# Products of zeros in TensorE's waits ahead of the first FFN group

## The chip, the cores and the metric

The kernel runs on one core of one Trainium2 chip. The metric is the device time of one execution in microseconds (us), as the median of several runs. The core's engines work side by side, each through its own queue in order: TensorE (PE in the profile; its weight loads are PEld), VectorE (DVE), ScalarE (ACT), GpSimd (POOL) and SyncE (SP). They wait for each other by semaphores, and the 16 DMA engines move data between HBM and the on-chip memory. TensorE writes its results to PSUM, which this kernel uses as eight banks of 128 x 512 float32.

TensorE's clock is granted by a throttle. The profile shows it as a share of full speed, 1.00 or 0.50 here.

## What is computed

Sliding-window attention with an ALiBi bias (8 batches, 8 heads, 576 positions, head size 64, window 128), and then a gated FFN over the 4608 resulting tokens:

```python
scores = scale * np.matmul(q, k.transpose(0, 1, 3, 2))
bias = slopes[:, None, None] * (-np.abs(rel).astype(np.float32))[None, :, :]
mask = (rel >= 0) & (rel < window)
scores = np.where(mask, scores + bias[None], -1000000000.0)
attn = np.exp(scores)            # after the row maximum was taken off
attn = attn / (np.sum(attn, axis=-1, keepdims=True) + 1e-09)
x = np.matmul(attn, v)           # then as 4608 tokens x 512
g = x @ w_gate                   # 512 x 1536
gelu = 0.5 * g * (1.0 + erf(g * inv_sqrt2))
out = (gelu * (x @ w_val)) @ w_out   # 1536 x 512
```

Inputs and output are float32 in HBM. The kernel computes in bfloat16 with float32 sums.

## The kernel before

The first FFN group of 512 tokens needs the attention of batch 0, and nothing can be computed before the first rows of q and k have landed. So the kernel has an opening, in which batch 0 goes through its stages with little beside it, and then a long steady part, in which the attention of later batches is spread between the FFN's products. The change touches only the opening. Its building blocks:

```python
def bank():                                   # one PSUM bank, from a pool of 8
    return psum.tile([128, 512], FP32, name="ps")

def transpose_runs(n, what, c, ps):           # q or k of two heads, on TensorE
    ...
            nc.tensor.transpose(out=ps[...], in_=src[...], identity=ident[...])

def scores(b, s, cs, then=None):              # for the head pairs in cs
    pss = []
    for c in cs:
        ps = [bank(), bank()]
        pss.append(ps)
        ...                                   # score(): qT x kT into the two banks
    if then:
        then()                                # more TensorE work, ahead of the exps
    for c, ps in zip(cs, pss):
        P = p_pool[s].tile([128, 2, 512], BF16, name="P")
        for i in (0, 1):
            exp(P[:, i, :], ps[i])            # ScalarE, L170
        mask(P..., emask...)                  # VectorE, L173: times exp(bias) and mask

def sums(b, s):                               # row sums: P x ones on TensorE, L221
    ps = bank()
    ...
    nc.vector.reciprocal(sumrow[b][:, lo:hi], ps[:, 0:hi - lo])         # L230

def spread_pe(b, s):                          # 1/sum to all partitions, L244
    pss = [bank() for _ in range(4)]
    ...                                       # four float32 products with sel
    for c, ps in enumerate(pss):
        copy = nc.scalar.copy if c % 2 == 0 else nc.vector.tensor_copy
        copy(out=recip[b][:, c, lo:hi], in_=ps[:, 0:hi - lo])           # L251

def values(b, s, cs):                         # P x v on TensorE, L262
    ...
    for c, ps in zip(cs, pss):
        nc.vector.tensor_tensor(out=xT[:, c, ...], in0=ps[...],
                                in1=recip[b][:, c, lo:hi], op=ALU.mult) # L268

def gate_val(g, f, lo=0, hi=512):             # gate and value of 128 FFN columns
    pg, pv = bank(), bank()
    ...                                       # 4 + 4 products with xT, L281
    nc.scalar.activation(out=gl, in_=pg, func=AF.Gelu)                  # L285
    nc.vector.tensor_tensor(out=hid[g][:, f, lo:hi], in0=pv, in1=gl, op=ALU.mult)  # L286
```

In `scores`, `s` is the part of the batch: 0 is positions 0 to 319, 1 is 320 to 575. The opening is this (the loads and constants ahead of it are cut down to what bears on the change):

```python
load_runs(0, 0, 4)                            # first rows of q and k, heads 0 to 3
nc.vector.memset(ident, 0.0)
...                                           # further memsets, masks, loads
for h in range(H):                            # emask: eight activations, L346
    nc.scalar.activation(out=emask[:, h, :], in_=tmpl, func=AF.Exp, scale=-slope)

def first(cs):
    for w in (0, 1):                          # q, then k
        for c in cs:
            ps = bank().bitcast(BF16)
            transpose_runs(0, w, c, ps)
            untangle(act if c == 3 else dve, 0, w, c, ps)   # copy to qT or kT, L136

def rest(cs, copy): ...                       # the same for the last 192 positions

first((0, 1))
scores(0, 0, (0, 1), lambda: first((2,)))
first((3,))
scores2(0)                                    # the middle blocks of all head pairs
scores(0, 0, (2, 3), lambda: rest((0, 1), dve))
scores(0, 1, (0, 1), lambda: sums(0, 0))
rest((2, 3), act)
scores(0, 1, (2, 3))
spread_pe(0, 0)
values(0, 0, range(4))
sums(0, 1)
for f in range(2):
    gate_val(0, f, 0, 320)
spread_pe(0, 1)
gate_val(0, 2, 0, 320)
values(0, 1, range(4))
for f in range(3):
    gate_val(0, f, 320, 512)
...
```

After that come the gates f = 3 to 11 of group 0 in full width, and the steady part.

Of the kernel before, what the change touches and what calls it, by code (L numbers as in the profile page):

```python
# [7 lines left out]
FP32 = mybir.dt.float32  # L8
BF16 = mybir.dt.bfloat16
# [17 lines left out]
def kernel(  # L27
# [10 lines left out]
    nc = tc.nc  # L38
# [11 lines left out]
    consts = ctx.enter_context(tc.tile_pool(name="consts", bufs=1))  # L50
# [9 lines left out]
    psum = ctx.enter_context(  # L60
        tc.tile_pool(name="psum", bufs=8, space=bass.MemoryType.PSUM))

    def bank():
        return psum.tile([128, 512], FP32, name="ps")

    wg = consts.tile([128, 4, DFF], BF16, name="wg")
    wv = consts.tile([128, 4, DFF], BF16, name="wv")
# [27 lines left out]
    def runs(t, n):  # L95
        first, parts, r = RUNS[n]
        lo = 1536 * n
        return t.rearrange("p j x -> p (j x)")[0:parts, lo:lo + 512 * r].rearrange(
            "p (h x) -> p h x", h=H)

    def load_runs(n, h0, h1):
        first, parts, r = RUNS[n]
        for t, src in ((qs[0], q), (ks[0], k)):
            nc.gpsimd.dma_start(  # L104
                out=runs(t, n)[:, h0:h1, :],
                in_=src[0][h0:h1, first:first + parts * r, :].rearrange(
                    "h (p r) d -> p h (r d)", r=r))
# [14 lines left out]
    def transpose_runs(n, what, c, ps):  # L122

        first, parts, r = RUNS[n]
        src = runs((qs, ks)[what][0], n)
        for x in range(r):
            for i in (0, 1):
                nc.tensor.transpose(
                    out=ps[64 * i:64 * i + 64, parts * x:parts * x + parts],
                    in_=src[:, 2 * c + i, 64 * x:64 * x + 64],  # L130
                    identity=ident[0:parts, 0:parts])

    def untangle(copy, n, what, c, ps):
        first, parts, r = RUNS[n]
        dst = by_pair((qT, kT)[what][0])[:, c, 64 + first:64 + first + parts * r]
        copy(out=dst.rearrange("p (x r) -> p x r", r=r),  # L136
             in_=ps[:, 0:parts * r].rearrange("p (r x) -> p x r", r=r))

    def transpose(b, what, c, copy):
        ps = bank().bitcast(BF16)  # L140
        for j in range(5):
            nc.tensor.transpose(  # L142
                out=ps[:, 128 * j:128 * j + 128],
                in_=(qs, ks)[what][b][:, j, 128 * c:128 * c + 128], identity=ident)
        copy(out=(qT, kT)[what][b][:, :, c, :],
             in_=ps[:, 0:640].rearrange("p (j t) -> p j t", t=128))
# [15 lines left out]
    def score(b, c, i, j, qj, n, ps, col):  # L162
        nc.tensor.matmul(  # L163
            out=ps[:, col:col + 128 * n].rearrange("p (n t) -> p n t", n=n),
            lhsT=blocks(kT, b, i, c, j, 1).rearrange("p n t -> p (n t)"),
            rhs=blocks(qT, b, i, c, qj, n),
            start=True, stop=True)

    def exp(dst, src):
        nc.scalar.activation(out=dst, in_=src, func=AF.Exp, scale=0.125)  # L170

    def mask(dst, m):
        nc.vector.tensor_tensor(out=dst, in0=dst, in1=m, op=ALU.mult)  # L173

    def scores2(b):

        P = p2_pool.tile([128, 4, 2, 128], BF16, name="P2")
        probs2[b] = P
        ps = [bank(), bank()]
        for c in range(4):  # L180
            for i in (0, 1):
                score(b, c, i, 2, 2, 1, ps[i], 128 * c)
        for i in (0, 1):
            exp(P[:, :, i, :], ps[i].rearrange("p (c n) -> p c n", c=4))
        mask(P.rearrange("p c i n -> p (c i) n"), emask[:, :, 0:128])

    def scores(b, s, cs, then=None):
# [6 lines that stand above are left out]
            for j, qj, n, col in (((0, 0, 2, 0), (1, 1, 2, 256)),  # L194
                                  ((4, 4, 1, 0), (2, 3, 1, 128), (3, 3, 2, 256)))[s]:
                for i in (0, 1):
                    score(b, c, i, j, qj, n, ps[i], col)
        if then:
            then()
        for c, ps in zip(cs, pss):  # L200
            P = p_pool[s].tile([128, 2, 512], BF16, name="P")
            probs[b, s, c] = P
            for i in (0, 1):
                exp(P[:, i, :], ps[i])
            mask(P.rearrange("p i (n x) -> p i n x", n=2),
                 emask[:, 2 * c:2 * c + 2, :].unsqueeze(2).to_broadcast((128, 2, 2, 256)))

    def prob(b, s, c, i, j, n):
        if (s, j) == (0, 2):
            return probs2[b][:, c, i, 0:n]  # L210
        return probs[b, s, c][:, i, PCOL[s][j]:PCOL[s][j] + n]
# [3 lines left out]
    def sums(b, s):  # L215

        ps = bank()
        for j, a, e in PIECES[s]:
            for i in (0, 1):
                for c in range(4):  # L220
                    nc.tensor.matmul(  # L221
                        out=ps[32 * c:32 * c + 32, a:e],
                        lhsT=ones[:, min(j, 1), i, :], rhs=prob(b, s, c, i, j, e - a),
                        start=(i == 0 and j == 2 * s), stop=(i == 1 and j == 2 * s + 2),
                        skip_group_check=True)
        if s == 0:
            sumrow[b] = r_pool.tile([128, S], FP32, name="r")
            recip[b] = r_pool.tile([128, 4, S], FP32, name="rb")
        lo, hi = PART[s]
        nc.vector.reciprocal(sumrow[b][:, lo:hi], ps[:, 0:hi - lo])  # L230
# [9 lines left out]
    def spread_pe(b, s):  # L240
        lo, hi = PART[s]
        pss = [bank() for _ in range(4)]
        for c, ps in enumerate(pss):
            nc.tensor.matmul(  # L244
                out=ps[:, 0:hi - lo],
                lhsT=sel[32 * c:32 * c + 32, :, :].rearrange("p i m -> p (i m)"),
                rhs=sumrow[b][32 * c:32 * c + 32, lo:hi], start=True, stop=True,
                tile_position=(32 * c, 0))
# [4 lines that stand above are left out]
    def values(b, s, cs):  # L253
        lo, hi = PART[s]
# [4 lines that stand above are left out]
            for j, a, e in PIECES[s]:  # L259
                for i in (0, 1):  # L260
                    h = 2 * c + i
                    nc.tensor.matmul(  # L262
                        out=ps[64 * i:64 * i + 64, a:e],
                        lhsT=vb[b % 2][:, j, 64 * h:64 * h + 64],
                        rhs=prob(b, s, c, i, j, e - a),
                        start=(j == 2 * s), stop=(j == 2 * s + 2), skip_group_check=True)
        for c, ps in zip(cs, pss):
            nc.vector.tensor_tensor(  # L268
                out=xT[:, c, b * S + lo:b * S + hi], in0=ps[:, 0:hi - lo],
                in1=recip[b][:, c, lo:hi], op=ALU.mult)  # L270
# [34 lines left out]


    load_runs(0, 0, 4)
    nc.vector.memset(ident, 0.0)
    for t in (qT[0], kT[0]):
        nc.vector.memset(by_pair(t)[:, :, 0:64], 0.0)  # L310
# [2 lines left out]
        out=ident, in_=ident, compare_op=ALU.not_equal, fill=1.0,  # L313
# [5 lines left out]
    for half, base, step, chan in ((0, 0, 1, -1), (1, -1, -1, 1)):  # L319
        t = tmpl[:, 128 * half:128 * half + 128]  # L320
        nc.gpsimd.affine_select(
            out=t, in_=t, compare_op=ALU.is_ge, fill=1e9,
            base=base, pattern=[[step, 128]], channel_multiplier=chan)
    load_runs(1, 0, 8)
    for c in range(4):
        nc.gpsimd.affine_select(
            out=sel, in_=sel, compare_op=ALU.not_equal, fill=1.0,
# [22 lines left out]
    act, dve = nc.scalar.copy, nc.vector.tensor_copy  # L350
    def first(cs):
        for w in (0, 1):
            for c in cs:
                ps = bank().bitcast(BF16)
                transpose_runs(0, w, c, ps)
                untangle(act if c == 3 else dve, 0, w, c, ps)

    def rest(cs, copy):
        for c in cs:
            for w in (0, 1):  # L360
                ps = bank().bitcast(BF16)
                transpose_runs(1, w, c, ps)
                untangle(copy, 1, w, c, ps)

    first((0, 1))
    scores(0, 0, (0, 1), lambda: first((2,)))
    first((3,))
    scores2(0)
    scores(0, 0, (2, 3), lambda: rest((0, 1), dve))
    scores(0, 1, (0, 1), lambda: sums(0, 0))  # L370
    rest((2, 3), act)
    scores(0, 1, (2, 3))
    spread_pe(0, 0)
    values(0, 0, range(4))
    sums(0, 1)
# [7 lines left out]
    for n in range(2):  # L383
        nc.gpsimd.dma_start(
            out=wo[:, 6 * n:6 * n + 6, :],
# [93 lines left out]
```

The softmax here doesn't subtract the row's maximum and nothing guards it: scores larger than these inputs give would overflow.

## Time and profile before

| | |
|---|---|
| median of 3 runs | 367.69 us (367.64 to 367.73) |
| span of the profiled execution | 365.5 us |
| granted TensorE clock, mean of the span | 0.985 |
| first product on TensorE | 5.05 us after the span's start |
| first gate products | 23.33 us |

The span runs from the first to the last instruction of the profiled execution. A page of the profile gives the busy time of each engine, and then the same in 40 slices (9.1 us each here), where a digit is the busy share in tenths and PEclk is the granted clock in tenths. A chain of waits follows the work that ended last back to what released each step. Other views list one engine's instructions in order of time, the busy time in chosen stretches, and groups of equal instructions with their mean duration. A busy TensorE isn't TensorE at its peak: products are pipelined, and at half the clock the same work is busy for longer.

### The profile page before, as it was taken

How to read it: one execution, taken by the hardware profiler on the slowest of the kernel's cores; microseconds unless marked ns; L12 is line 12 of the kernel's file. 1: busy time of each engine (PE TensorE's matmuls, PEld its weight loads, DVE VectorE, ACT ScalarE, POOL GpSimd, SP SyncE). 2: the span in 40 equal slices, each digit the busy share in tenths (PEclk: the TensorE clock that was granted, in tenths of full speed). 3: DMA queues.
4: the chain of work that ended last, by engine and by line, in shares of the span. 5: the costliest groups of instructions: out<-in, count | busy, mean ns of one | idle time of the engine just before them, and what ended most of it. 6: DMA issues, size and time to landing. Idle time of an engine off the chain costs nothing.

```text
span 365.5 us, 6601 instructions
## 1 busy us (share of the span) xinstructions
PE 347.8 (95%) x2614; PEld 171.3 (47%) x2656; DVE 188.6 (52%) x306; ACT 187.3 (51%) x339; POOL 107.9 (30%) x140
## 2 busy tenths in 40 slices
PE   3799999999999999999999999999999999999995
PEld 2455545444454445444445444444444444444442
DVE  4794448543695469475547454655564404302320
ACT  5863487434966376943783368436842223323321
POOL 8945859913519202900850040000000000000000
PEclk9779999999999999999999999999999999999999
DMA  9999999999969994999991992094205020011002
GB/s 103 136 199 178 177 163 184 174 153 200 162 116 121 136 92 81 143 103 217 127 196 50 228 97 89 33 221 53 87 32 131 0 109 7 0 60 58 0 29 88
DMA packets 151168, 41.41 MB, mean 113 GB/s; under 512 B 138816, under 2 KB 144448, under 8 KB 151136
## 3 DMA queue, kind: packets, MB, share of 16 engines
q0 software_dynamic: 112608, 18.88, 67.8%
q1 hardware_dynamic: 38528, 22.10, 27.2%
q8 instruction: 21, 0.34, 0.4%
q14 instruction: 11, 0.09, 0.1%
HBM read 42.47 MB, written 9.51 MB: 142 GB/s over the span
## 4 chain that ended last, share of the span: by engine, by line
PE 86%; ACT 5%; DVE 3%; DMA 3%; issue 1%; POOL 1%; POOLq 0%; SPq 0%; ACTq 0%; DVEq 0%
PE ps L281 50%; PE ps L297 23%; PE ps L262 4%; ACT P L170 4%; PE ps L163 4%; DMA qT<-qs 3%; PE ps L221 2%; PE ps L244 2%; DVE r L230 1%; DVE P L173 1%; DVE xT L268 1%; ACT emask L346 1%; PE ps L142 1%; POOL ks L104 0%; ACT L170 0%
## 5 line engine op out<-in xcount | busy, mean ns | idle before, releaser
L286 DVE TENSOR_TENSOR hT<-ps,gelu 128x512 bf16<-128x512 f32 (+2 forms) x111 | 74.3, 674 | 121.9 <-PE ps L281 109.3
L285 ACT ACTIVATE gelu<-ps 128x512 bf16<-128x512 f32 (+2 forms) x111 | 64.9, 585 | 119.6 <-PE ps L281 117.2
L281 PE MATMUL ps<-xT,wg 128*128 128x512 bf16 (+2 forms) x430 | 110.6, 374 | 0.8
L281 PE MATMUL ps<-xT,wv 128*128 128x512 bf16 (+2 forms) x435 | 110.4, 373 | 0.6
L297 PE MATMUL ps<-wo,hT 128*128 128x512 bf16 x413 | 97.2, 380 | 1.5 <-issue 0.6
L170 ACT ACTIVATE P<-ps 128x512 bf16<-128x512 f32 x144 | 74.4, 632 | 7.1 <-PE ps L163 7.0
L281 PEld LDWEIGHTS <-wv 128*128 128x128 bf16 x444 | 43.3, 98 | 50.3 <-issue 0.2
L281 PEld LDWEIGHTS <-wg 128*128 128x128 bf16 x444 | 41.9, 98 | 48.9 <-issue 1.1
L173 DVE TENSOR_TENSOR P<-P,emask 128x1024 bf16<-128x1024 bf16 x72 | 48.3, 685 | 31.3 <-ACT P L170 31.0
L297 PEld LDWEIGHTS <-hT 128*128 128x128 bf16 x432 | 39.8, 98 | 49.0 <-issue 4.4
L84 POOL DMA_DIRECT2D vb<-in_v_dram x40 | 33.7, 862 | 75.8 <-PE ps L262 75.0
L302 ACT COPY osb<-ps 128x512 f32<-128x512 f32 x36 | 21.7, 603 | 37.2 <-PE ps L297 32.8
L84 POOL DMA_DIRECT2D qs<-in_q_dram x35 | 29.6, 877 | 24.9 <-DMA qT<-qs 12.9
L230 DVE RECIPROCAL r<-ps 128x320 f32<-128x320 f32 (+1 forms) x16 | 30.7, 1939 | 3.1 <-PE ps L221 3.1
L84 POOL DMA_DIRECT2D ks<-in_k_dram x35 | 29.6, 887 | 6.4 <-DMA qs<-in_q_dram 3.0
L163 PE MATMUL ps<-qT,kT 64*128 64x256 bf16 (+1 forms) x384 | 24.0, 254 | 3.0 <-DVE kT L136 1.3
L268 DVE TENSOR_TENSOR xT<-ps,rb 128x320 bf16<-128x320 f32 (+1 forms) x64 | 24.7, 449 | 0.8 <-DMA rb<-rd 0.8
L163 PEld LDWEIGHTS <-kT 64*128 64x128 bf16 x384 | 13.1, 96 | 16.9 <-issue 11.6
L262 PE MATMUL ps<-P,vb 128*64 128x128 bf16 (+2 forms) x384 | 19.4, 251 | 0.1
L262 PEld LDWEIGHTS <-vb 128*64 128x64 bf16 x384 | 15.4, 113 | 7.3 <-issue 7.2
L221 PE MATMUL ps<-P,ones 128*32 128x128 bf16 (+2 forms) x384 | 11.6, 256 | 1.3 <-DVE P L173 1.3
L221 PEld LDWEIGHTS <-ones 128*32 128x32 bf16 x384 | 8.5, 101 | 5.6 <-issue 4.5
(47 smaller groups left out, 91.3 us busy)
## 6 DMA issues: line engine op xcount, KB each, us to landing
out_dram<-osb SPq DMA_DIRECT2D x36, 256.0 KB, 2.7
rb<-rd SPq DMA_DIRECT2D x8, 576.0 KB, 7.1
vb<-in_v_dram POOLq DMA_DIRECT2D x32, 128.0 KB, 4.7
qs<-in_q_dram POOLq DMA_DIRECT2D x28, 128.0 KB, 6.7
ks<-in_k_dram POOLq DMA_DIRECT2D x28, 128.0 KB, 6.4
wg<-in_moe_w_gate_dram POOLq DMA_DIRECT2D x4, 384.0 KB, 11.0
wv<-in_moe_w_val_dram POOLq DMA_DIRECT2D x4, 384.0 KB, 12.2
wo<-in_moe_w_out_dram POOLq DMA_DIRECT2D x2, 768.0 KB, 10.9
```

The source lines that it names most:

```text
L84: nc.gpsimd.dma_start(out=t[lo:128, j, :].rearrange("p (h d) -> p h d", h=H), in_=src[b][:, 128 * j - 64 + lo:128 * j + 64, :].rearrange(" ...
L163: nc.tensor.matmul(out=ps[:, col:col + 128 * n].rearrange("p (n t) -> p n t", n=n), lhsT=blocks(kT, b, i, c, j, 1).rearrange("p n t -> p ( ...
L170: nc.scalar.activation(out=dst, in_=src, func=AF.Exp, scale=0.125)
L173: nc.vector.tensor_tensor(out=dst, in0=dst, in1=m, op=ALU.mult)
L221: nc.tensor.matmul(out=ps[32 * c:32 * c + 32, a:e], lhsT=ones[:, min(j, 1), i, :], rhs=prob(b, s, c, i, j, e - a), start=(i == 0 and j == ...
L230: nc.vector.reciprocal(sumrow[b][:, lo:hi], ps[:, 0:hi - lo])
L262: nc.tensor.matmul(out=ps[64 * i:64 * i + 64, a:e], lhsT=vb[b % 2][:, j, 64 * h:64 * h + 64], rhs=prob(b, s, c, i, j, e - a), start=(j == ...
L268: nc.vector.tensor_tensor(out=xT[:, c, b * S + lo:b * S + hi], in0=ps[:, 0:hi - lo], in1=recip[b][:, c, lo:hi], op=ALU.mult)
L281: nc.tensor.matmul(out=ps[:, 0:hi - lo], lhsT=w[:, c, 128 * f:128 * (f + 1)], rhs=xT[:, c, t0 + lo:t0 + hi], start=(c == 0), stop=(c == 3))
L285: nc.scalar.activation(out=gl[:, 0:hi - lo], in_=pg[:, 0:hi - lo], func=AF.Gelu)
L286: nc.vector.tensor_tensor(out=hid[g][:, f, lo:hi], in0=pv[:, 0:hi - lo], in1=gl[:, 0:hi - lo], op=ALU.mult)
L297: nc.tensor.matmul(out=po, lhsT=hid[g][:, f, 128 * t:128 * (t + 1)], rhs=wo[:, f, :], start=(f == 0), stop=(f == NF - 1))
```

## The change

A tile of zeros, 128 x 512 in bfloat16, is added, and a helper that issues a given number of products of zeros ahead of the next bank's real work. Each has 128 x 128 zeros as its weights and 512 columns of zeros, and writes to the bank that the real work then overwrites (`start=True`), so the results stay what they were. There are 26 of them: 9 ahead of the first transposes of q, 2 ahead of those of k, 2 ahead of the first scores, 1 ahead of the transposes of the third head pair, 2 ahead of the scores of the last two pairs, 4 ahead of the first scores of part 1, 2 ahead of the sums, 1 ahead of the last scores, and 3 ahead of the first spread. They are meant to fill TensorE's waits ahead of the first FFN group, so that the throttle doesn't halve its clock there. Nothing is taken away.

```diff
+    heat = [0]
+
     def bank():
-        return psum.tile([128, 512], FP32, name="ps")
+        ps = psum.tile([128, 512], FP32, name="ps")
+        for _ in range(heat.pop()):
+            nc.tensor.matmul(out=ps, lhsT=zeros[:, 0:128], rhs=zeros, start=True, stop=True)
+        heat.append(0)
+        return ps
+
+    def keep_busy(n):
+        heat[0] = n
...
     load_runs(0, 0, 4)
+    zeros = consts.tile([128, 512], BF16, name="zeros")
+    nc.vector.memset(zeros, 0.0)
     nc.vector.memset(ident, 0.0)
...
     def first(cs):
         for w in (0, 1):
+            if w and len(cs) == 2:
+                keep_busy(2)
             for c in cs:
...
+    keep_busy(9)
     first((0, 1))
-    scores(0, 0, (0, 1), lambda: first((2,)))
+    keep_busy(2)
+    scores(0, 0, (0, 1), lambda: (keep_busy(1), first((2,))))
     first((3,))
     scores2(0)
+    keep_busy(2)
     scores(0, 0, (2, 3), lambda: rest((0, 1), dve))
-    scores(0, 1, (0, 1), lambda: sums(0, 0))
+    keep_busy(4)
+    scores(0, 1, (0, 1), lambda: (keep_busy(2), sums(0, 0)))
     rest((2, 3), act)
+    keep_busy(1)
     scores(0, 1, (2, 3))
+    keep_busy(3)
     spread_pe(0, 0)
     values(0, 0, range(4))
     sums(0, 1)
```

## The prediction

> **What bounds the kernel now.** I read the page's busy shares first. TensorE is the bound over the whole span.
>
> ```profile
> span 365.5 us, 6601 instructions
> PE 347.8 (95%) x2614; PEld 171.3 (47%) x2656; DVE 188.6 (52%) x306; ACT 187.3 (51%) x339; POOL 107.9 (30%) x140
> PEclk9779999999999999999999999999999999999999
> ```
>
> The clock row has a dent in slices 2 and 3 (9 to 27 us), and this is what the change aims at. An average over a stage says little, so next I read the stretches of this opening. Columns: stretch and length, then busy us with instructions of PE, PEld, DVE, ACT, POOL, then the granted clock.
>
> ```profile
> 10.00:13.40 3.40, 1.85 (x34) 1.16 (x32) 2.17 (x6) 3.08 (x8) 3.40 (x5) 0.99 1.70 118
> 13.40:16.80 3.40, 2.79 (x44) 1.78 (x46) 2.19 (x7) 3.04 (x6) 3.40 (x6) 0.50 1.75 129
> 16.80:20.20 3.40, 2.89 (x34) 1.39 (x30) 3.40 (x4) 3.04 (x8) 2.06 (x3) 0.50 1.24 182
> 20.20:23.60 3.40, 3.40 (x54) 2.49 (x51) 3.40 (x9) 2.05 (x4) 1.58 (x2) 0.50 1.29 197
> 23.60:27.00 3.40, 3.40 (x29) 2.16 (x28) 2.95 (x5) 1.42 (x4) 1.49 (x2) 1.00 1.31 203
> ```
>
> The clock is halved from 13.4 to 23.6 us, 10.2 us in all, and the drop follows a stretch in which TensorE was busy for 1.85 of 3.40 us. Yet ACT was busy for 3.08 and 3.04 us of the stretches around the drop, and DVE for all 6.8 us from 16.8 to 23.6. A halved clock costs time only where TensorE is what the others wait for. So the view that decides is the chain of waits through this opening (start us, length us, what):
>
> ```profile
> 5.77 2.56 ACT emask L346 x8
> 8.33 1.93 ACT P L170 x4
> ...
> 14.20 1.21 DVE P L173 x2
> 15.41 0.04 issue
> 15.46 1.13 PE ps L221 x19
> 16.59 0.02 issue
> 16.61 2.17 DVE r L230
> 18.78 0.14 issue
> 18.91 1.45 PE ps L244 x8
> 20.37 2.06 PE ps L262 x24
> 22.43 0.97 PE ps L221 x19
> 23.40 2.40 PE ps L281 x16
> 25.80 0.64 PE ps L244 x8
> ```
>
> Up to 15.4 us the chain is ScalarE and VectorE. From 15.46 it alternates: row sums on TensorE, a reciprocal on VectorE, then 5 us of TensorE at half clock. A naive reading halves every TensorE piece of that. The timeline of VectorE shows a second chain just beside it, and this is the step on which my number turns:
>
> ```profile
> 18.68 2.43 DVE L173 TENSOR_TENSOR P<-P,emask 128x1024 bf16<-128x1024 bf16 x4
> 21.03 0.88 DVE L251 COPY rb<-ps 128x320 f32<-128x320 f32 x2
> 21.83 1.68 DVE L268 TENSOR_TENSOR xT<-ps,rb 128x320 bf16<-128x320 f32 x4
> ```
>
> The reciprocal, four masks, two copies and four products stand in this order in VectorE's queue and run without a gap from 16.61 to 23.51 us. The first gate products (from 23.33) need all four of these products' results.
>
> [...]
>
> One warning on the clock figure: it reads 1.00 from the start, but the groups of instructions deny that. A score of 256 columns took 404 ns between 5 and 10 us, 269 ns between 10 and 13.3, and 417 ns between 13.7 and 23.3. So TensorE was slow up to about 10 us as well, for which the trace just has no record.
>
> **The change, part by part.** *Added:* 26 products of 512 columns, 9+2+2+1+2+4+2+1+3, and one memset of 128x512 bf16 (the 64x512 bf16 memsets took 0.27 us). Nothing is removed, and no transfer is touched. At full clock the fill costs 26 x 0.216 = 5.6 us of TensorE, at half clock 11.2 us.
>
> *The nine* stand ahead of the first transposes, for which TensorE now waits until 5.05 us on the load of q. The memset can be done near 1.1 us; at half clock nine take 9 x 0.432 = 3.9 us, so they end about when the load lands: cost up to 0.1 us. *The next two* fill the 0.29 us wait on k. [...] ScalarE has the eight emask activations until 8.33 anyway, so a first score by 8.3 costs nothing.
>
> *The next nine* (2+1+2+4) stand where ScalarE and VectorE set the pace: ten activations run from 11.33 to 16.44 without a gap, and the masks end at 15.41. The fill takes 0.2 to 0.9 us at a time, in waits of 0.68, 0.99 and 0.2 us and the slack of a faster clock. I count 0. *Two* ahead of the sums: at full clock the last scores are done by about 14.75, the zeros by 15.2, and the sums wait on the mask at 15.41 either way.
>
> *What the clock gives.* The 21 sums take 1.12 us now; the same 21 at full clock, in a later group, took 0.66. So the reciprocal starts 0.46 us earlier, at 16.15. The next scores wait on ScalarE's copies, whose start moves from 16.92 to about 16.5; *one* zero fits there. The last scores end near 17.7, the *three* zeros take 0.65 and end at 18.35, and the reciprocal ends at 16.15 + 2.17 = 18.32. So spread starts at about 18.45 instead of 18.91 and takes 0.75 (a later group) instead of 1.45. The values and sums shrink by about 1.0 and 0.4 us. TensorE alone would gain 0.46 + 0.70 + 1.03 + 0.42 = 2.6 us, and some more in the first gates.
>
> But VectorE's queue moves by 0.46 us and no more: its products end at 23.51 - 0.46 = 23.05. The first gate's fourth product waits for that, then 0.135 us a product at full clock (320 columns; 4 in 0.54): the three remaining sets of four of f=0 and f=1 run from 23.2 to 24.82. Before, the second spread started at 25.73. VectorE's second reciprocal (1.76 us) now runs from 23.0 to 24.75, so spread starts at about 24.9. Gain: 25.73 - 24.9 = 0.83 us. Behind it everything was already at full clock and TensorE leads: the gain is carried on.
>
> *Is it lost later?* The weights: GpSimd's wait on the landing of the first wv quarter ends at 22.50, and its first use moves from 24.00 to 23.2: 0.7 us left. The k of the next batch: its small packets end near 40.3 us, its transposes start at 41.9: 1.6 us left. wo lands 9.4 and 12.3 us after its issues at 36.7 and 37.6, and the two halves are first used at 50.6 and after 52.9. The transfers behind q's transposes of the third batch land at 84.8 and are used at 90.1. None is eaten up by 0.8 us. So 367.69 - 0.83 + about 0.05 for the nine and the three that end a little late = 366.9.
>
> **Rivals.** *Whole TensorE gain (2.6 us or more, 365.0).* For it: the chain names TensorE for most of 15.5 to 26 us. Against it: VectorE has no gap from 16.61 to 23.51, and its work gets no faster with TensorE's clock. *The fill doesn't hold the clock.* In the stretch from 10.0 to 13.4 the scores and transposes stream about 1.0 us of columns; the two zeros and two of the four add 0.86, making 1.9 of 3.4. The stretch from 16.8 to 20.2 had TensorE busy for 2.89 us and the clock stayed halved, so I can't exclude that 1.9 is too little. Then the four zeros take 1.7 us instead of 0.9 and delay the scores by about 0.9, and the three take 1.3 and push spread from 18.9 to about 20: slower by 1 to 1.5 us, 369. *The start is late.* If the clock comes up only at 8 us, the eleven zeros at half clock delay the first scores beyond 8.33, and ScalarE's unbroken chain moves by 0.3 to 0.5 us: 367.3. *Full clock, but the shift meets a load:* 0.7 us of weights' slack caps it; no change to the point.
>
> **Range and chances.** About 65% for the clock held and VectorE as the limit (366.4 to 367.2), 15% for the late start or a part of the fill on the path (367.2 to 367.9), 17% for a clock that still falls (367.9 to 369), and a few per cent for more than 1.4 us. So 366.9, and 8 in 10 between 366.1 and 368.2. A change of 2% is 7.35 us; the fill at half clock throughout is 11 us but over half of it in waits, and all that the clock could give is half of 10.2 us. Hence 0.01 faster, 0.98 within, 0.01 slower.
>
> **What would show it.** Right: a clock of 1.00 from 13.4 to 23.6; the first reciprocal near 16.1 and its masks, copies and products gapless to about 23.0; spread for the second part near 24.9; the continuous gates from 31.77 starting near 31.0. Wrong: VectorE idle ahead of its products with xT (TensorE still leads, or fill on the path); a clock of 0.50 anywhere after 8 us; the first P activations after 8.4 us; TensorE waiting for wv or for ks that it did not wait for.

## The result

The changed kernel takes 366.86 us (median of 6 runs, 366.56 to 367.72) against 367.72 us for the kernel before beside it (367.64 to 367.99): a ratio of 0.9977, interval 0.9965 to 0.9990. It is faster by about 0.86 us, 0.2%, as the prediction of 366.9 us had it.

The page after:

```profile
span 364.9 us, 6652 instructions
PE 351.6 (96%) x2638; PEld 170.7 (47%) x2682; DVE 189.0 (52%) x307; ACT 187.2 (51%) x339; POOL 108.1 (30%) x140
PEclk9999999999999999999999999999999999999999
```

The dent in the clock row is gone. TensorE is busy for 3.8 us more (351.6 against 347.8), which is not useful work: the fill adds to its busy time, and the real work, at the whole clock, takes less (the first spread 0.82 us instead of 1.45). The same stretches as before, with the same columns (stretch, length, busy PE, PEld, DVE, ACT, POOL, clock):

```profile
13.40:16.80 3.40, 3.33 (x58) 1.62 (x56) 2.65 (x7) 3.40 (x9) 3.40 (x6) 1.00 1.72 124
16.80:20.20 3.40, 3.24 (x45) 1.81 (x47) 3.40 (x5) 3.35 (x10) 2.29 (x4) 1.00 1.28 190
20.20:23.60 3.40, 2.37 (x37) 1.22 (x34) 3.40 (x8) 1.37 (x2) 1.39 (x2) 1.00 1.31 202
```

In the last stretch TensorE, which was busy throughout before, is busy for 2.37 of 3.40 us. It got its work done sooner and waits. What for stands in its timeline (start, length, engine, line, operation; in brackets the idle time before and what ended it):

```profile
18.50 0.82 PE L255 MATMUL ps<-r,sel 32*128 32x320 f32 x8
...
20.36 0.96 PE L232 MATMUL ps<-P,ones 128*32 128x128 bf16 x24
22.02 1.40 PE L292 MATMUL ps<-xT,wg 128*128 128x320 bf16 x4 [0.69 <-DVE xT L279]
...
24.97 0.71 PE L255 MATMUL ps<-r,sel 32*128 32x256 f32 x8
```

The first four gate products waited 0.69 us for xT, and then were drawn out over 1.2 us, since each needs the next product of VectorE. VectorE's queue after:

```profile
16.17 2.16 DVE L241 RECIPROCAL r<-ps 128x320 f32<-128x320 f32 x1 [0.74 <-PE ps L232]
18.25 2.43 DVE L184 TENSOR_TENSOR P<-P,emask 128x1024 bf16<-128x1024 bf16 x4
20.59 0.88 DVE L262 COPY rb<-ps 128x320 f32<-128x320 f32 x2
21.39 1.68 DVE L279 TENSOR_TENSOR xT<-ps,rb 128x320 bf16<-128x320 f32 x4
```

Set against the times of before (16.61, 18.68, 21.03 and 21.83 us), each start is 0.43 or 0.44 us earlier and each length is the same. The whole clock moved the start of this queue, by the shorter sums (all 24 in 0.99 us, where the last 21 alone took 1.12 before), and nothing else in it. The lead at the second spread is 25.73 - 24.97 = 0.76 us. It doesn't all reach the end. The chain of waits further on, after (start, length, what):

```profile
31.02 10.09 PE ps L292 x46
41.11 0.68 PE ps L153 x10
...
42.06 1.46 PE ps L292 x6
```

Before, the same steps were these:

```profile
31.77 10.09 PE ps L281 x46
41.86 0.56 PE ps L142 x10
...
42.69 1.46 PE ps L281 x6
```

The lead is 0.75, 0.75 and then 0.63 us: ten transposes of batch 1's q and k, which took 0.56 us before, take 0.68. From there on the lead stays at 0.62 to 0.63 us to the end of the chain, and the two spans differ by as much (365.5 and 364.9).

### The profile page after: what moved, and what is told of

It is laid out like the page before. It is cut to its first block, busy times and chain, and to the rows that moved or that the text cites. A ratio compares the mean times of both kernels' runs of the same rounds, so it can differ in the third digit from the quotient of the medians.

```text
span 364.9 us, 6652 instructions
## 1 busy us (share of the span) xinstructions
PE 351.6 (96%) x2638; PEld 170.7 (47%) x2682; DVE 189.0 (52%) x307; ACT 187.2 (51%) x339; POOL 108.1 (30%) x140
## 4 chain that ended last, share of the span: by engine, by line
PE 86%; ACT 8%; DVE 2%; issue 1%; POOL 1%; POOLq 0%; ACTq 0%; DVEq 0%
PE ps L292 50%; PE ps L308 23%; ACT P L181 6%; PE ps L273 4%; PE ps L174 4%; PE ps L232 2%; PE ps L255 1%; DVE xT L279 1%; DVE P L184 1%; ACT L181 1%; ACT emask L359 1%; PE ps L153 1%; DVE r L241 0%; POOL ks L115 0%; ACT osb L313 0%
## 5 line engine op out<-in xcount | busy, mean ns | idle before, releaser
L273 PE MATMUL ps<-P,vb 128*64 128x128 bf16 (+2 forms) x384 | 18.4, 243 | 0.1
L232 PE MATMUL ps<-P,ones 128*32 128x128 bf16 (+2 forms) x384 | 10.8, 243 | 1.3 <-DVE P L184 1.1
```

Of the source, the lines that this page charges most:

```text
L232: nc.tensor.matmul(out=ps[32 * c:32 * c + 32, a:e], lhsT=ones[:, min(j, 1), i, :], rhs=prob(b, s, c, i, j, e - a), start=(i == 0 and j == ...
L273: nc.tensor.matmul(out=ps[64 * i:64 * i + 64, a:e], lhsT=vb[b % 2][:, j, 64 * h:64 * h + 64], rhs=prob(b, s, c, i, j, e - a), start=(j == ...
```

## The experiments

The theory: with the clock held, VectorE's queue sets when the first gates come, and a part of what is won is taken back where batch 1's k has not landed yet. The rival: TensorE is the only limit, so that the fill brought all that the clock can give. All ratios are to the kernel before on the same chip, with 95% intervals. The runs are from more than one chip, on which the kernel before took 367.84 us (rows 2 to 5), 367.75 us (the two halves and the last two rows) and 367.59 us (the other three), so medians of different groups can be compared only roughly.

| kernel | median us (range, runs) | ratio |
|---|---|---|
| changed kernel | 366.86 (366.56 to 367.72, 6) | 0.9977 (0.9965 to 0.9990) |
| + late transposes | 366.79 (366.52 to 367.58, 11) | 0.9974 (0.9964 to 0.9983) |
| + VectorE relieved | 366.85 (366.14 to 367.31, 8) | 0.9970 (0.9958 to 0.9981) |
| + both | 365.57 (365.25 to 368.90, 14) | 0.9944 (0.9928 to 0.9959) |
| no fill, both | 367.80 (367.09 to 368.70, 14) | 0.9996 (0.9987 to 1.0005) |
| + late transposes, mask only | 366.39 (366.27 to 366.89, 6) | 0.9959 (0.9943 to 0.9975) |
| + late transposes, copies only | 366.00 (365.77 to 366.51, 5) | 0.9951 (0.9937 to 0.9965) |
| only the early fill | 367.73 (367.01 to 368.09, 13) | 0.9995 (0.9987 to 1.0003) |
| only the late fill | 368.02 (366.55 to 368.68, 14) | 1.0004 (0.9992 to 1.0016) |
| six ahead of the spread | 366.78 (366.56 to 367.49, 8) | 0.9977 (0.9967 to 0.9987) |
| half of the columns | 367.05 (366.54 to 368.17, 22) | 0.9979 (0.9971 to 0.9987) |
| transposes as fill | 367.17 (366.54 to 368.30, 18) | 0.9982 (0.9973 to 0.9991) |

### Late transposes

```diff
-            if g == 0 and f >= 8:
+            for c in {9: (0,), 10: (1, 2), 11: (3,)}.get(f, ()) if g == 0 else ():
                 for w in (0, 1):
-                    transpose(1, w, f - 8, (act, dve)[w])
+                    transpose(1, w, c, (act, dve)[w])
```

> With the fill, and the transposes of batch 1's q and k one gate later (after gates 9, 10, 10 and 11 instead of 8 to 11). If the k load takes back a part of the gain (in the changed kernel TensorE was 0.75 us ahead at 31 us and 0.63 us from 42 us on) and is also what makes its runs scatter by 1.1 us: the 0.75 us stay to the end, about 366.6 us to 366.8, and the runs lie within 0.4 us. Rival, the 0.12 us are something else and the scatter is the clock's: 366.9 and a scatter as before.

366.79 us: too near to the changed kernel to tell 0.12 us by the medians. In the profile the transposes take 0.56 us again. No view of the changed kernel's profile names a wait on a load at these transposes, so that the load of k took back the 0.12 us is inferred here; the next experiment shows the wait itself. The runs scatter by 1.1 us as before, not within 0.4 us: this load is not what makes them scatter.

### VectorE relieved

```diff
-    scores(0, 1, (0, 1), lambda: (keep_busy(2), sums(0, 0)))
+    later = []
+    scores(0, 1, (0, 1), lambda: (keep_busy(2), sums(0, 0, later)), lambda: later[0]())
...
-            copy = nc.scalar.copy if c % 2 == 0 else nc.vector.tensor_copy
+            copy = nc.scalar.copy if c % 2 == 0 or (b, s) == (0, 0) else nc.vector.tensor_copy
```

In the helpers, `sums` puts its reciprocal into `later`, and `scores` calls it after its first mask.

> With the fill, and VectorE relieved by about 1.4 us in the opening: one mask goes ahead of the reciprocal into VectorE's wait, and two copies of the first spread go to ScalarE. If VectorE's queue held back the first gates: their fourth product starts near 21.8 instead of 23.1 us, the value product then waits for the load of wv at 22.0 to 22.5, the second spread comes near 24.2 instead of 24.97, 0.75 us earlier; but then batch 1's k isn't there at 40.5, TensorE waits for it until 41.2, and nearly nothing is left: 366.5 to 366.9 us. Rival, TensorE alone set the end: no change of the second spread, 366.9 us. Second rival, no wait on k: 366.1 us.

366.85 us, no better than the changed kernel, and yet the rival falls by the profile: the second spread starts at 23.95 instead of 24.97, 1.0 us earlier. This is where that went, in the timeline of TensorE:

```profile
23.95 0.71 PE L260 MATMUL ps<-r,sel 32*128 32x256 f32 x8
...
40.20 0.53 PE L153 MATMUL ps<-ident,ks 128*128 128x128 bf16 x3
41.38 0.23 PE L153 MATMUL ps<-ident,ks 128*128 128x128 bf16 x1 [0.66 <-DMA ks<-in_k_dram]
42.22 0.23 PE L153 MATMUL ps<-ident,ks 128*128 128x128 bf16 x1 [0.60 <-DMA ks<-in_k_dram]
```

TensorE came 1.0 us earlier to k's transposes (40.20 instead of 41.23) and waited 1.26 us there. The profiled run, at 367.31 us, is the longest of the eight, and the shortest took 366.14 us, so not every run need lose all of it; the median does. An experiment read by its time alone would have said that VectorE doesn't matter.

### Both

The two edits together, nothing else.

> Both: VectorE relieved, and the transposes one gate later. If VectorE's queue and then the k load are the two limits: about 1.5 us ahead of the kernel before, 366.1 to 366.3 us. If the k load isn't a limit: the same as the relief alone. If VectorE isn't: the same as the late transposes alone, 366.7 us.

365.57 us, better than expected: 0.9944 is 2.1 us of 367.84 (2.3 by the medians). One of the 14 runs took 368.90 us. The mean clock recorded for it is 0.995, the lowest of the 14, so the clock may have fallen in it; no profile of that run is kept. The chain of waits of the profiled run shows VectorE for 1.3 us only:

```profile
20.85 1.28 DVE xT L284 x3
...
22.17 1.93 PE ps L297 x13
24.10 0.64 PE ps L260 x8
...
30.07 10.74 PE ps L297 x49
```

The long run of gates starts at 30.07 us, 0.95 earlier than in the changed kernel, though the first P activation came 0.2 us later in this run; and nothing takes it back. With the late transposes in both, VectorE's relief is worth 366.79 - 365.57 = 1.22 us; without them, nothing that the runs can tell (0.9970 against 0.9977, with intervals that overlap).

### Both, without the fill

> The kernel before, without the fill, with VectorE relieved and the transposes one gate later. If TensorE's half clock and VectorE's queue end within 0.1 to 0.3 us of each other there, relief alone gives little: the clock stays halved from 13.4 to 23.6 us, 367.4 to 367.7 us. Rival, VectorE alone was the limit and the clock hardly matters: 1 us or more is gained without any fill, 366.7 us or less.

367.80 us, a ratio of 0.9996 with 1 inside its interval. The clock in its stretches:

```profile
16.80:20.20 3.40, 2.90 (x45) 1.78 (x37) 3.00 (x3) 2.67 (x9) 2.44 (x4) 0.50 1.27 184
20.20:23.60 3.40, 3.40 (x52) 2.22 (x48) 2.95 (x6) 3.25 (x7) 1.24 (x2) 0.50 1.31 201
```

Now VectorE has gaps (3.00 and 2.95 us busy of 3.40) and TensorE has none at the end. So at half the clock TensorE's own work sets the end once VectorE is relieved, and the two had ended close together before. From the first product of the first sums to the second spread this kernel takes 26.33 - 15.38 = 10.95 us, and the kernel before took 25.73 - 14.80 = 10.93 us: no gain. The clock alone brought 0.9 us, VectorE's relief and the late transposes without it nothing that can be told from 0, and all together 2.1 to 2.3.

### The two halves of the relief

Only the mask ahead of the reciprocal, or only the two copies on ScalarE, each with the fill and the late transposes.

> The fill, the late transposes, and of VectorE's relief only the first half: one mask ahead of the reciprocal instead of behind it, 0.6 us less in VectorE's queue between the reciprocal and the products with xT. VectorE as the limit: the second spread 0.6 us earlier than with the late transposes alone, about 366.2 us. Rival, the copies alone made the gain: 366.8 us.

> The fill, the late transposes, and only the other half of the relief: the two copies on ScalarE. VectorE's queue is 0.8 us shorter, but ScalarE's four copies end 1.44 us after its last exp, near 20.8, and VectorE's masks at 20.6, so its products end at about 22.3 instead of 23.07: 0.7 us earlier, about 366.1 us. Together with the mask the gain was 1.2 us and not 1.3, as the wv load then ends the wait; so the two halves should nearly add up. Rival, only the mask counts: 366.8 us.

366.39 and 366.00 us, so 0.40 and 0.79 us below the late transposes alone. But these runs are from another chip; by the ratios it is 0.6 and 0.8 us, against 1.1 us for both, and each ratio is uncertain by about 0.5 us. The profiles can be compared better, from the first product of the first sums to the second spread, which leaves out when the first k landed: 24.96 - 15.14 = 9.82 us with the late transposes alone, 24.68 - 15.33 = 9.35 with the mask, 24.16 - 15.13 = 9.03 with the copies and 24.03 - 15.48 = 8.55 with both. The halves save 0.47 and 0.79 us, together 1.26, and both save 1.27. The mask gave less than the 0.6 expected: in its profile the three masks behind the reciprocal take 1.95 us and not three quarters of 2.43 (1.82), as the last one has to wait for the exp that ends at 19.65. That is the 0.13 us that are missing.

### Only the early, only the late fill

Early only:

```diff
     scores2(0)
-    keep_busy(2)
     scores(0, 0, (2, 3), lambda: rest((0, 1), dve))
-    keep_busy(4)
-    scores(0, 1, (0, 1), lambda: (keep_busy(2), sums(0, 0)))
+    scores(0, 1, (0, 1), lambda: sums(0, 0))
     rest((2, 3), act)
-    keep_busy(1)
     scores(0, 1, (2, 3))
-    keep_busy(3)
```

Late only keeps these, and drops the ones ahead of them:

```diff
-            if w and len(cs) == 2:
-                keep_busy(2)
...
-    keep_busy(9)
     first((0, 1))
-    keep_busy(2)
-    scores(0, 0, (0, 1), lambda: (keep_busy(1), first((2,))))
+    scores(0, 0, (0, 1), lambda: first((2,)))
```

> Only the first 14 products of zeros (9, 2, 2 and 1, ahead of 9 us), none of the later 12. [...] Rival, one good start is enough: clock whole through to 24 us and 366.9 us.

> Only the later 12 products of zeros (2, 4, 2, 1, 3, from 11 us on), none of the first 14. The kernel before had a whole clock from 10 to 13.4 us without any fill. If what counts is only that the stretch after 10 us is busy enough, the clock stays whole and the gain is kept: 366.9 us, and the early 14 are needless. If the zeros before 10 us are needed: the clock falls at 13.4 us, the 12 run at half clock and cost 0.5 to 1.5 us, 368 to 369 us.

Early only, 367.73 us, as without any fill. Its clock was whole by k's transposes at 7.18 us (0.53 us, against 0.85 in the kernel before) and fell again (the first of these lines is the mean over the fall, the last over the rise):

```profile
13.40:16.80 3.40, 2.14 (x36) 1.26 (x36) 2.43 (x7) 3.36 (x7) 3.40 (x6) 0.89 1.84 145
16.80:20.20 3.40, 2.90 (x37) 1.69 (x36) 3.28 (x4) 2.72 (x8) 2.65 (x4) 0.50 1.27 189
20.20:23.60 3.40, 3.40 (x55) 2.41 (x52) 3.40 (x9) 2.37 (x4) 1.10 (x3) 0.61 1.31 199
```

From the means it is halved from about 16.0 to 22.9 us, and that this is shorter than the 10.2 us of before is no help, as this stretch holds the spread and the values (1.45 and 2.13 us, as before). So one good start isn't enough; the recorded mean clock of all 13 runs is 0.984 to 0.991.

Late only, 368.02 us, with a scatter of 2.1 us: three runs at 366.55 to 366.97, the others from 367.55 up to 368.68. The profiled run took 368.64 us, and shows what a clock that isn't up yet makes of the fill:

```profile
14.03 1.89 PE L70 MATMUL ps<-zeros 128*128 128x512 bf16 x4
15.85 1.04 PE L174 MATMUL ps<-qT,kT 64*128 64x128 bf16 x12
```

The four products of zeros took 1.02 us in the changed kernel and 1.89 here, and the scores behind them start at 15.85 instead of 13.94. The three short runs may be those in which the clock came up in time, but no profile of one is kept. The clock figure of this profile reads 1.00 in this very stretch, which can't be what was granted there. The kernel before is alike: the first record of the clock in its trace is at 9.95 us, and the figure reads 1.00 ahead of it, though a score of 256 columns took 404 ns there and 269 ns after it.

### Six products of zeros ahead of the spread

```diff
-    keep_busy(3)
+    keep_busy(6)
     spread_pe(0, 0)
```

> The changed kernel with 6 instead of 3 products of zeros ahead of the first spread. The 3 end at about the reciprocal's end, so three more stand on the path: 3 x 0.216 = 0.65 us later for the first spread. TensorE then has 0.7 us of wait on VectorE's products in hand (the values and sums end at 21.3 and the gates wait until 22.0 and 23.1), but the spread's copies lead to these products: VectorE's copies start when its masks end at 20.6, and spread would end at 19.9. So no or less than 0.2 us of loss: 366.9 to 367.1 us. Rival, TensorE leads there: plus 0.65, 367.5 us.

366.78 us, no loss:

```profile
19.16 0.82 PE L255 MATMUL ps<-r,sel 32*128 32x320 f32 x8
...
21.93 1.49 PE L292 MATMUL ps<-xT,wg 128*128 128x320 bf16 x4 [0.29 <-DVE xT L279]
```

The spread starts 0.66 us later (18.50 before), and TensorE's wait on xT shrinks from 0.69 to 0.29 us: idle time is all it cost. VectorE's products with xT start at 21.40 us (21.39 in the changed kernel) and the second spread at 24.98 (24.97). This shows that TensorE doesn't lead there.

### Half of the columns, and transposes as fill

```diff
-            nc.tensor.matmul(out=ps, lhsT=zeros[:, 0:128], rhs=zeros, start=True, stop=True)
+            nc.tensor.matmul(out=ps[:, 0:256], lhsT=zeros[:, 0:128], rhs=zeros[:, 0:256], start=True, stop=True)
```

> The changed kernel with products of zeros of 256 instead of 512 columns, 26 of them, half of the fill. The late part of the fill adds 1.9 us of columns to the 7 us after 10 us, and half is 0.95. If the fill has a margin, the clock stays whole and the time is 366.9 us or a little less; if it was just enough, the clock falls near 13 to 16 us in all or some of the runs, and the median lies near 367.6 us with a wide scatter.

In the other kernel the first nine stay products, and each of the 17 later ones becomes four of these:

```diff
+                nc.tensor.transpose(out=ps.bitcast(BF16)[:, 128 * x:128 * x + 128],
+                                    in_=zeros[:, 0:128], identity=ident)
```

> The changed kernel with the first nine as they are, and each of the 17 later products of zeros replaced by four transposes of zeros of 128 columns. If transposes don't count as work for the clock: it is halved again at about 13 to 16 us as with the early part of the fill alone, and the transposes cost like the fill or more, 367.7 us or above. If they count like products: clock whole to 24 us and 366.9 us.

Half the columns: 367.05 us, ratio 0.9979.

```profile
12.14 0.90 PE L174 MATMUL ps<-qT,kT 64*128 64x256 bf16 x8
...
18.82 0.82 PE L255 MATMUL ps<-r,sel 32*128 32x320 f32 x8 [0.22 <-DVE r L241]
```

The clock came up later (these eight scores took 0.61 us in the changed kernel), but then it was held: the spread took 0.82 us (1.45 in the kernel before). So in this run half of the late fill was enough to hold the clock, while half of the early fill was not enough to bring it up as soon. Transposes as fill: 367.17 us, ratio 0.9982, and the clock is held too, at 1.00 from 13.4 to 23.6 us:

```profile
13.80 1.05 PE L74 MATMUL ps<-ident,zeros 128*128 128x128 bf16 x16
...
19.34 0.82 PE L260 MATMUL ps<-r,sel 32*128 32x320 f32 x8
```

The twelve scores behind these sixteen transposes took 0.71 us, against 0.74 in the changed kernel and 1.14 in the kernel before, and the spread took 0.82. The early fill alone lost the whole clock soon after, at about 16.0 us, so the transposes kept it; and 15 of the 18 runs have a recorded mean clock of 0.998 or more, where no run with the early fill alone is above 0.991. The runs fall into two heaps, 366.54 to 366.71 and 367.00 to 368.30. The profiled one is of the second (367.37 us): in it k landed late, its transposes started at 7.59 us instead of 6.57, the first P activation came at 9.05 us instead of 8.35, and the second spread at 25.80 instead of 24.97.

## Why the prediction was right

- *The clock.* Right: in the profiled run it was whole from about 6 us on: the nine products of zeros took 0.63 us each, the two at 5.88 us 0.38, as the four at 12.98 did, and k's transposes 0.53 us instead of 0.85. The rival of a clock that still falls holds for the early fill alone, and for part of the runs of the late fill alone: up to 1.1 us of loss (368.68 us against the median of 367.59 before it), where 1 to 1.5 were named; by its ratio the late fill alone is no different from the kernel before. In the runs with a mean of 0.995 (see below) the clock may have fallen with the whole fill too.
- *The fill in the waits costs nothing.* Right. q's transposes followed the nine at 5.16 us, k's transposes started at 6.57 instead of 6.20, the first scores at 7.58 instead of 7.39, and the first P activation at 8.26 instead of 8.24. The 0.216 us counted for a product of 512 columns at the whole clock is what the gates of the kernel before show, where four advance by 0.865 us; the 0.432 at half clock is twice that, an estimate, and the starts of the nine lay 0.42 us apart. The three ahead of the spread let it start at 18.50 (18.45).
- *VectorE's queue as the limit.* Right, and the step on which the number turned. The reciprocal came at 16.17 (16.15), the products ended at 23.07 (23.05), the second spread came at 24.97 (24.9), the continuous gates at 31.02 (31.0). Six zeros and the relief show it as a cause.
- *The rival of 2.6 us.* Wrong for this kernel. VectorE's relief and the late transposes on top of the fill came to 2.1 to 2.3 us of it.
- *"1.6 us left" for the k of the next batch.* Wrong. I took the end of the bulk of small packets, near 40.3 us, for the landing. Small packets went on: from 41.0 to 41.5 us the kernel before still moved 15 of them, though the trace doesn't say of which load, and with VectorE relieved the last wait on k ended only at 42.22 us. The slack before was about 0.6 us (0.75 - 0.12), so 0.12 of the 0.75 us went there, and in the profiled run with VectorE relieved its whole gain. TensorE waiting for k where it had not waited before was one of the signs named for a wrong prediction; it came true, too small to move the number.
- *0.83 - 0.05.* The sum of 0.78 stands against 0.63 in the profiled runs and 0.86 by the medians. The interval of the ratio (0.9965 to 0.9990) is a gain of 0.4 to 1.3 us, so that the median came within 0.04 us of 366.9 is in part luck; the starts of the steps, each within 0.1 us, say more for the mechanism.
- *Transposes as fill.* The expectation left open whether they count as work for the clock. 68 transposes of zeros in place of 17 products kept it: it read 1.00 from 13.4 to 23.6 us, where the early fill alone had it at 0.50 from about 16.0 to 22.9. Whether transposes alone would also raise it wasn't tried, as the first nine stayed products.

*What stays open:* the scatter of about 1 us. One part is the landing of the first k: its transposes started at 6.20 us in the profile with the late transposes (366.52 us) and at 7.59 in that with transposes as fill (367.37 us), after a wait of 0.71 us for the load, and there everything up to the second spread came 0.8 us later. Another may be the clock. A mean of 0.995 is what 3.7 us at half clock in 366 give (an estimate, 2 x 0.005 x 366). It stands beside the longest run with the late transposes (367.58 us), with six zeros (367.49) and with both edits (368.90), and beside three runs with transposes as fill (367.50 to 367.56); where the clock fell in them isn't known, as no profile of one is kept. In the kernel before, the mean shows a fall like the profiled one (0.985) in only 15 of the 106 runs taken beside the experiments; the other 91 read 0.998 to 1.000 and are no faster on average. As the figure reads 1.00 ahead of the first record too (9.95 us in the profile of the kernel before), it can't be told from the mean whether their clock was whole.

## What to carry to other kernels

A halved clock costs only where TensorE is what the others wait for (in the kernel before, 10.2 us at half clock; keeping it whole brought 0.9 us): lay the queue of the next engine beside TensorE's chain before counting the gain, and relieve both: the fill alone brought that 0.9 us, the relief and the late transposes without it nothing, and all together 2.1 to 2.3. Idle products in TensorE's waits cost nothing here where each fitted its wait (six instead of three ahead of the spread: 366.78 us against 366.86), but the fill had to run through to where the clock was needed: the early part alone took 367.73 us, with the clock at 0.50 again from about 16.0 us. And when a step comes earlier, compare its new time with the landing of the last packet of each load that it needs, not with the bulk.

## What the hardware showed beside this

With 26 products of zeros the granted clock read 1.00 from 13.4 to 23.6 us, where it read 0.50 without, and with 68 transposes of zeros in place of 17 of them it read 1.00 there too. The fall didn't come at a fixed time after the kernel's start: it came at 13.4 us in the kernel before, at about 14.0 in its version with both edits (its clock's mean from 13.4 to 16.8 us was 0.59, so 0.18 of these 3.4 us were still at full speed), and at about 16.0 with the early fill alone. It lasted about 10.2 us in the first two and 6.8 us in the third. In the second the opening's work ran 0.6 us later as well, so these runs don't tell a fall that follows the work from one that follows a clock of its own.
